# A fixed, searched order for the first two groups of an attention + MLP kernel, and the unread products at its end left out

## The chip, the cores and the metric

One core of a Trainium2 chip. The metric is the device time of the kernel in microseconds, the median of several runs. Five engines take part: TensorE (PE in the profile; its weight loads are PEld), VectorE (DVE), ScalarE (ACT), GpSimd (POOL) and SyncE (SP), which here issues almost every DMA. Each engine works through its own instructions in the order in which the program lists them; semaphores make one wait for another.

## The reference

Block-wise linear attention over q, k, v of shape (4, 8, 768, 64), all float32, with a decay per head, and then a two-layer MLP with leaky ReLU; the weights arrive as float64.

```
intra = einsum('bhic,bhjc->bhij', qb, kb) * Dmask          # scores, masked by lam**(i-j)
intra = einsum('bhij,bhjd->bhid', intra, vb)
inter = einsum('bhid,bhde->bhie', qb * lam_pow, kv_state)  # from the running state
kv_state = lam_block * kv_state + einsum('bhsd,bhse->bhde', kb_dec, vb)
...
x = attn_out.transpose(0, 2, 1, 3).reshape(3072, 512)
h = x @ w_in            # 512 -> 2048
g = maximum(0.01*h, h)
out = g @ w_out         # 2048 -> 512
```

## The kernel before, in words

The 3072 tokens are cut into 24 chunks of 128 (six per batch), and four chunks make a group of 512 tokens, so there are six groups. The 2048 hidden columns are cut into eight pairs p of 256.

Every float32 product of the MLP is made from three products of rounded parts: each operand is split into a high part h, a low part l and a mixed part m, and TensorE multiplies h by h, l by l and m by m. `up(g, p)` (L628 to L664) multiplies group g by weight pair p: two half blocks of 128 columns, three passes (h, l, m) of four 512-wide matmuls each, all on L640. Between l and m ScalarE scales the accumulator (L658), after m it applies the leaky ReLU into a buffer `gs` (L661), and a DMA stores `gs` to the DRAM array `g` (L664). The second half of the kernel, `down` (L700), reads these back and makes the output; nothing of it is touched by the change.

For chunk c the attention part is: load k, q, v (L338, L388); transpose k and q on TensorE (L403; four transposes each, here called Tk and Tq) and copy them out on ScalarE (L414, L415); scores (`go`) and state products (`kv`) on TensorE (L313); mask them (`sc`, L452) and update the running state (`st`) on VectorE (L457, L459) with POOL scaling between (L462); POOL or VectorE scales k (L419) and q (`qsT`, L423); outputs (`own`, then `inter` in two parts with a small probe read of `po` between, L491) on TensorE; and the split into xh (ScalarE, L507), xl and xm (VectorE, L508, L510). From chunk 10 on, q and k are not transposed on TensorE but loaded in 32 small strided pieces per run of chunks (`load_subs`, L374) and turned on VectorE.

A weight pair p arrives as two halves of float64 (L566, 512 KB each). ScalarE reads each half three times (L578, L580, L582), VectorE shifts and adds (L584, L585) to make float32, and `parts` makes wh (ScalarE L591 or VectorE L593), wl (VectorE L596) and wm (VectorE L602).

The order of all this is not written out by hand. The class `Plan` (L37 to L159) collects operations with an engine (or several to choose from), an estimated length, what they read and write as string keys, and a rank. `emit` then simulates the engines: again and again it takes the operation that can start first, ties broken by rank. An operation is known by its number in the order in which it was added. `seq` (L738 on) sets the ranks. At the start, where TensorE would sit idle by the plan's estimate, `busy` issues dummy transposes of 128x128 (L266) into the bank b10, until that bank is first used by a product. Before everything it issues eleven of them.

The steps that matter around the change, with their numbers: 71 to 73 load k3, q3, v3; 94 and 100 the two halves of the weights of p=1, 165 and 171 of p=0, 203 and 209 of p=2, 323 and 329 of p=4; 95 to 97 ScalarE's three reads of 94; 168 its third read of 165; 106, 177, 215, 335 make wh of p = 1, 0, 2, 4; 80 and 81 are kv and go of chunk 3, 87, 88, 90 its outputs, 91 its xh; 113 and 122 the transposes of q4 and q5; 154 the first pass of `up(0, 1)`; 243 the store of `up(0, 0)`; 266 the load of k8.

After the last operation the kernel issues 32 more matmuls that nobody reads: 24 in strips of the array (`strips`, L802) and eight small ones (L809).

Of the kernel before, what the change touches and what calls it, by code (L numbers as in the profile page):

```python
# [34 lines left out]


class Plan:  # L37

# [6 lines left out]
    def __init__(self):  # L45
        self.ops, self.last, self.rank = [], {}, 0.0
        self.chain, self.chains = None, {}
        self.warm, self.slack, self.more = 0.0, 0.0, {}
        self.first = {"PE": 0.0, "ACT": 0.0, "DVE": 3.4, "POOL": 0.0, "DMA": 0.2}
        self.cold, self.idle, self.spare = 6.0, None, None  # L50

    def begin(self, name):
# [30 lines left out]
    def emit(self):  # L83
        n = len(self.ops)
        follows, heads = {}, {}
        for c in self.chains.values():
# [26 lines left out]
        done = []  # L113
        while len(done) < n:
            best = None
            for e in free:
                for i in able[e]:
                    if e == "PE" and (i != locked[0] if locked else i in follows):
                        continue
                    t = max(free[e], since(i, e))  # L120
                    if (best is None or (t, self.ops[i][3]) < best[:2]) and good(i, e, t):
                        best = (t, self.ops[i][3], i, e)
            t, _, i, e = best
            ways, fn = self.ops[i][:2]
            if i in heads:
                locked = list(heads[i])
            elif locked and i == locked[0]:
                locked.pop(0)
            for x in ways:
# [8 lines left out]
            for u in users[i]:  # L138
                ends[u].append((free[e] + self.more.get(i, 0.0), e))
                left[u] -= 1  # L140
                if not left[u]:
                    for x in self.ops[u][0]:
                        able[x].add(u)
        self.timeline = sorted(done)

# [3 lines left out]
        for t, _, i, e in self.timeline:  # L149
            ways, fn, deps = self.ops[i][:3]  # L150
            t = max([soon[e]] + [over[d][0] + (0.0 if over[d][1] == e != "DMA" else self.SOON[over[d][1]]) for d in deps])
            if e == "PE":
                if self.spare in self.ops[i][4]:
# [9 lines left out]
def kernel(  # L163
# [32 lines left out]
    GOFIRST = 3  # L196
    SUBL, FIRST = 0.75, -8.0

    DV = 10
# [22 lines left out]

    W = [[sb([P, 4 * 2 * P], f"w{x}{p}", F32R) for x in "hlm"] for p in range(NP)]
    X = [[sb([P, KO, T], f"x{x}{i}", F32R) for x in "hlm"] for i in range(2)]
# [22 lines left out]
    kqv = [[x[:, i * H * D:(i + 1) * H * D].rearrange("p (h d) -> p h d", h=H) for i in range(2)] for x in kqv_f]  # L247
    kTs, qTs, qsTs = ([part(HP * C).rearrange("p (y t) -> p y t", y=HP) for _ in range(2)] for _ in range(3))
    sc = part(2 * HP * C2).rearrange("p (x y t) -> p x y t", x=2, y=HP)
    state = [part(HP * D).rearrange("p (y d) -> p y d", y=HP) for _ in range(4)]  # L250
# [75 lines left out]
    def of(c):  # L326
        return c // NCB, c % NCB, c % 2

# [98 lines left out]
    def scores(c):  # L427
# [17 lines left out]
        if c < GOFIRST:  # L445
            add("PE", 0.47, go, [f"kT{i}", f"qT{i}"], ["psc"])
        add("PE", 0.47, kv, [f"k{i}", f"v{i}"], ["psc"])
        if c >= GOFIRST:
            add("PE", 0.47, go, [f"kT{i}", f"qT{i}"], ["psc"])

        def uses():
            add("DVE", 0.69, lambda: nc.vector.tensor_tensor(sc, psc[:, :, lower, :], decay, op=ALU.mult), ["psc", "fk"], ["sc"])  # L452
            for t in range(n_pu):
                j = 2 * c + t
                new = state[j % 4]
                if n == 0 and t == 0:
                    add("DVE", 0.42, lambda new=new: nc.vector.tensor_copy(new, pu[0]), ["psc"], [f"st{j % 4}"])  # L457
                else:
                    add("DVE", 0.42, lambda new=new, t=t: nc.vector.tensor_tensor(new, new, pu[t], op=ALU.add),  # L459
                        ["psc"], [f"st{j % 4}"])  # L460
# [126 lines left out]
    def parts(p, src, keys):  # L587
        wh, wl, wm = W[p]
        def head(e):
            if e == "ACT":  # L590
                nc.scalar.activation(out=wh, in_=src, func=AF.Copy, bias=0.0, scale=NEAR / S)  # L591
            else:
                nc.vector.tensor_scalar(wh, src, NEAR / S, None, op0=ALU.mult)  # L593

        add(("ACT", "DVE"), (1.05, 0.7), head, keys, [f"wh{p}"])
        add("DVE", 1.25, lambda: nc.vector.scalar_tensor_tensor(wl, wh.bitcast(F32), -S, src, op0=ALU.mult, op1=ALU.add),  # L596
            keys + [f"wh{p}"], [f"wl{p}"])
        difference(p)

    def difference(p):  # L600
        wh, wl, wm = W[p]
        add("DVE", 1.25, lambda: nc.vector.scalar_tensor_tensor(wm, wl.bitcast(F32), 1.0, wh.bitcast(F32), op0=ALU.mult, op1=ALU.subtract),  # L602
            [f"wh{p}", f"wl{p}"], [f"wm{p}"])

    def w_in(p):
        for h in range(2):
            to_float32("wi", p, h, w32[:, h, :], f"w32{h}")
        parts(p, w32f, ["w320", "w321"])

# [153 lines left out]
    for n, x in enumerate(seq):  # L763
# [15 lines left out]
        elif x[0] == "wp":  # L779
            if not freed:  # L780
                add("DVE", 0.0, lambda: None, [], ATT + [f"gr{j}" for j in range(NR)])
                add("ACT", 0.0, lambda: None, [], [f"raw{j}" for j in range(NRAW)] + ["t0", "t1"])
# [5 lines left out]
        else:  # L788
            down(*x[1:])
    plan.emit()  # L790


    a, b = ring[0][0], W[0][0]
    spare = acc[0] + acc[1]

    def strips(n, times):

        k = P // n
        for _ in range(times):
            for i in range(n):  # L800
                r = slice(i * k, (i + 1) * k)
                nc.tensor.matmul(spare[i], lhsT=a[r, 0:P], rhs=b[r, 0:T], start=True, stop=True, skip_group_check=True)  # L802

    strips(2, 6)
    strips(4, 3)
    f = graw[0]
    for _ in range(4):
        for i in range(2):
            nc.tensor.matmul(spare[2][HALF[i], 0:C2], lhsT=f[:, 0:C2], rhs=f[:, 0:C2], start=True, stop=True, skip_group_check=True)  # L809

# [29 lines left out]
```

## Time and profile before

| what | value |
|---|---|
| median of 3 runs | 611.09 us (611.05 to 611.78) |
| profiled execution: span from first to last instruction | 610.3 us; its own time is not listed apart |
| TensorE busy | 601.9 us, 99% of the span |
| VectorE, ScalarE, POOL busy | 313.2, 269.9, 86.6 us |
| mean granted clock of TensorE | 0.997 |
| first product of `up` (L640) | 30.41 us after the start |
| dummy transposes (L266) | 30 |
| last product of `down` (L700) | issued by 606.3 us |
| DMA moved | 105.18 MB, 172 GB/s mean |

The profile names an instruction by engine, line and the tiles it writes and reads (`b<-xh,wh`). Busy time says where an engine had work; a wait says what ended an idle stretch; the chain of waits follows the last instruction back through what released each step. Rows by window give the busy microseconds of each engine in a stretch, the granted clock of TensorE (1.00 is full) and the share of the DMA engines in use.

### The profile page before, as it was taken

To read this page: it belongs to the slowest core of one execution; us is meant where nothing else is said; L and a number is where in the kernel's file an instruction comes from. 1 tells how busy PE (TensorE), PEld (TensorE's weight loads), DVE (VectorE), ACT (ScalarE), POOL (GpSimd) and SP (SyncE) were. 2 spreads that over 40 slices of the span, in tenths; PEclk is the share of its full clock that TensorE was granted. 3 is DMA by queue.
4 is the path that set the end of the run, shared out by engine and by line. 5 is a ranking of instruction groups with operands and counts; after the bars stand their busy time and mean duration, and the time that the engine had idled before them with its cause. 6 is when DMAs were issued, how large, how long until landed. Compare 5 with 4: busy or idle time off the path is not lost.

```text
span 610.3 us, 13012 instructions
## 1 busy us (share of the span) xinstructions
PE 601.9 (99%) x5426; PEld 497.6 (82%) x5426; DVE 313.2 (51%) x418; ACT 269.9 (44%) x430; POOL 86.6 (14%) x90
## 2 busy tenths in 40 slices
PE   7799999999999999999999999999999999999999
PEld 5688888888888878888788888888888888888887
DVE  5899764334243426326366755545454544636531
ACT  4678974444455646555577522222222313214111
POOL 2564412114133004104000000000000000000000
PEclk9899999999999999999999999999999999999999
DMA  9999775666889878886686843524333343333201
GB/s 201 236 261 263 215 204 126 175 154 176 192 212 245 212 222 219 212 242 212 233 302 219 278 155 103 173 69 139 137 104 134 111 136 111 132 104 126 82 1 69
DMA packets 147754, 105.18 MB, mean 172 GB/s; under 512 B 123632, under 2 KB 124400, under 8 KB 147696
## 3 DMA queue, kind: packets, MB, share of 16 engines
q1 hardware_dynamic: 147552, 104.36, 58.8%
q8 instruction: 42, 0.69, 0.5%
q14 instruction: 16, 0.13, 0.1%
q10 hardware_dynamic: 144, 0.00, 0.0%
HBM read 68.69 MB, written 35.65 MB: 171 GB/s over the span
## 4 chain that ended last, share of the span: by engine, by line
PE 95%; DMA 2%; ACT 1%; DVE 1%; issue 0%; SPq 0%; ACTq 0%
PE b L640 42%; PE b L700 18%; PE po L700 11%; PE psc L700 11%; PE po L313 4%; PE psc L313 4%; PE pt L700 4%; DMA g<-gs 1%; DMA att<-in_v_dram 1%; PE pt L403 1%; DMA att<-in_q_dram 1%; PE po L403 0%; PE psc L802 0%; ACT att L415 0%; PE b L266 0%
## 5 line engine op out<-in xcount | busy, mean ns | idle before, releaser
L682 ACT ACTIVATE xh<-att 128x1024 fp32r<-128x1024 f32 x48 | 50.8, 1060 | 149.1 <-PE b L700 133.6
L683 DVE SCALAR_TENSOR_TENSOR xl<-att,xh 128x1024 fp32r<-128x1024 f32 x48 | 58.7, 1223 | 97.5 <-ACT xh L682 97.5
L640 PE MATMUL b<-xm,wm 128*128 128x512 f32 (+2 forms) x392 | 104.5, 392 | 0.7 <-ACT b L658 0.7
L640 PE MATMUL b<-xh,wh 128*128 128x512 f32 (+2 forms) x392 | 103.2, 386 | 0.8 <-ACT xh L507 0.8
L640 PE MATMUL b<-xl,wl 128*128 128x512 f32 (+2 forms) x392 | 103.4, 387 | 0.0
L640 PEld LDWEIGHTS b<-xh,wh 128*128 128x128 f32 x392 | 72.9, 188 | 16.0 <-ACT xh L507 0.9
L640 PEld LDWEIGHTS b<-xl,wl 128*128 128x128 f32 x392 | 72.7, 188 | 15.1 <-DVE wl L596 0.3
L640 PEld LDWEIGHTS b<-xm,wm 128*128 128x128 f32 x392 | 71.4, 188 | 16.0 <-ACT b L658 1.1
L658 ACT ACTIVATE b<-b 128x512 f32<-128x512 f32 (+2 forms) x97 | 56.1, 580 | 60.6 <-PE b L640 60.5
L661 ACT ACTIVATE gs<-b 128x512 f32<-128x512 f32 (+2 forms) x97 | 57.0, 592 | 44.2 <-PE b L640 38.3
L700 PE MATMUL b<-wh,xh 128*128 128x512 f32 x192 | 74.7, 389 | 0.0
L700 PE MATMUL b<-wl,xl 128*128 128x512 f32 x192 | 74.7, 389 | 0.0
L685 DVE SCALAR_TENSOR_TENSOR xm<-xl,xh 128x1024 fp32r<-128x1024 f32 x48 | 58.7, 1225 | 4.7
L462 POOL TENSOR_TENSOR att<-att 128x256 f32<-128x256 f32 x40 | 34.4, 861 | 58.7 <-DVE att L459 58.7
L700 PEld LDWEIGHTS b<-wh,xh 128*128 128x128 f32 x192 | 36.1, 188 | 7.5
L700 PEld LDWEIGHTS b<-wl,xl 128*128 128x128 f32 x192 | 36.0, 188 | 7.5
L423 POOL TENSOR_TENSOR att<-att 128x512 f32<-128x512 f32 (+1 forms) x20 | 25.3, 1265 | 95.6 <-PE po L313 34.7
L452 DVE TENSOR_TENSOR att<-psc,att 128x512 f32<-128x512 f32 x24 | 16.5, 689 | 43.1 <-PE psc L313 43.1
L584 DVE TENSOR_SCALAR w<-w 128x512 int32<-128x512 int32 x32 | 19.6, 612 | 36.0 <-ACT w L578 35.9
L700 PE MATMUL psc<-wh,xh 128*128 128x512 f32 x96 | 37.3, 389 | 0.0
L700 PE MATMUL psc<-wl,xl 128*128 128x512 f32 x96 | 37.3, 389 | 0.0
L700 PE MATMUL psc<-wm,xm 128*128 128x512 f32 x96 | 37.3, 389 | 0.0
(79 smaller groups left out, 810.4 us busy)
## 6 DMA issues: line engine op xcount, KB each, us to landing
att<-g SPq DMA_DIRECT2D x48, 512.0 KB, 3.3
g<-gs SPq DMA_DIRECT2D x47, 512.0 KB, 4.0
raw<-in_moe_w_in_dram SPq DMA_DIRECT2D x16, 512.0 KB, 5.5
raw<-in_moe_w_out_dram SPq DMA_DIRECT2D x16, 512.0 KB, 4.8
att<-in_k_dram SPq DMA_DIRECT2D x48, 128.0 KB, 4.3
att<-in_v_dram SPq DMA_DIRECT2D x24, 256.0 KB, 4.5
out_dram<-gs SPq DMA_DIRECT2D x23, 256.0 KB, 2.1
wo<-w SPq DMA_DIRECT2D x8, 512.0 KB, 5.9
```

Source lines behind the costliest of these rows:

```text
L313: nc.tensor.matmul(dst[HALF[cols]], lhsT=lhsT[HALF[rows]], rhs=rhs[HALF[rows]], start=start, stop=True, skip_group_check=True)
L423: add(eng, us, lambda: e.tensor_tensor(o, x, _bc(pow_q, 2, 2)[:, :, m, :], op=ALU.mult), ["fq", dep], [f"qsT{i}"])
L452: add("DVE", 0.69, lambda: nc.vector.tensor_tensor(sc, psc[:, :, lower, :], decay, op=ALU.mult), ["psc", "fk"], ["sc"])
L462: add("POOL", 0.7, lambda new=new, j=j: nc.gpsimd.tensor_tensor(state[(j + 1) % 4], new, _bc(lam_c, 2, D), op=ALU.mult), [f"st{j % 4}", "f ...
L584: add("DVE", 0.42, lambda: nc.vector.tensor_scalar(d, d, 3, None, op0=ALU.logical_shift_left), [], [key])
L640: nc.tensor.matmul(dst, lhsT=w[z][:, kk * 2 * P + f * P:kk * 2 * P + (f + 1) * P], rhs=x[z][:, kk, toks], start=start and kk == 0, stop=kk ...
L658: add("ACT", ns, lambda b=b: nc.scalar.activation(out=b, in_=b, func=AF.Copy, bias=0.0, scale=S + 1.0), [], [kb], rank=-1.5)
L661: add("ACT", ns, lambda b=b, r=r: nc.scalar.activation(out=r, in_=b, func=AF.Prelu, bias=0.0, scale=1.0 / WS, alpha=0.01), [kb], [f"gs{jg} ...
L682: add("ACT", 1.05, lambda: nc.scalar.activation(out=h, in_=graw[j], func=AF.Copy, bias=0.0, scale=NEAR), reads, wr("h"))
L683: add("DVE", 1.25, lambda: nc.vector.scalar_tensor_tensor(l, graw[j], 1.0, h.bitcast(F32), op0=ALU.mult, op1=ALU.subtract), reads + [f"rh{ ...
L685: add("DVE", 1.25, lambda: nc.vector.scalar_tensor_tensor(m, l.bitcast(F32), -S, h.bitcast(F32), op0=ALU.mult, op1=ALU.add), [f"rh{j}", f" ...
L700: nc.tensor.matmul(acc[tb][z // 2][:, cols], lhsT=ring[j][z][:, f * T + tb * P:f * T + (tb + 1) * P], rhs=W[pp][z][:, f * d_model:(f + 1) ...
```

## The change

The 707 operations numbered 0 to 706 are no longer ordered by the plan. They are all operations that were added up to the last `up` of group 1: attention of chunks 0 to 11 and the products of chunk 12's round that belong to it, all eight weight pairs of w_in, all sixteen `up` of groups 0 and 1, and the loads for the turned chunks up to 15. A list, `ORDER`, gives their order; a suffix a, v or p picks ScalarE, VectorE or POOL where there is a choice, and `fN` puts N dummy transposes ahead of the next TensorE operation. `emit` first places the listed operations as they stand and then goes on by its old rule; the automatic dummies are off. What the list does to each engine's own order can be read off the numbers: on SP's queue q1 goes ahead of k1, 94 directly behind k1, v3 (73) directly behind k3, k8 (266) ahead of 323 and 329, 243 behind them. On TensorE go of chunk 3 goes ahead of kv, Tq of chunks 4 and 5 behind the outputs of chunk 3, and the chunks' rounds from 8 on stand at other places among the products. ScalarE reads 94 twice before the copy of chunk 1's k; 106, 177 and 215 are on ScalarE, 335 is on VectorE. Sixteen dummies are listed, where the plan had put in nineteen.

The key `psc` is split into `psS` (scores) and `psK` (state products), so the plan no longer orders these two against each other; `factors_q` reads the key it depended on. `OWN`, which would give some chunks buffers inside the weight tiles, is empty. The 32 unread matmuls at the end are gone.

```diff
+ORDER = """
+2 3 4 0 26 f3 5 25 9v f2 6 1 94 8 7 10 f5 11 12 28 14 48 13 15 29 95 32v 49 96 18 33 27 19 30 16 20a 31 100 17
+f1 21 50 22 34 23 51 72 36 52 53 55 24 54 97 f2 35 41 37 71 56 42 38 101 57 98 43a 102 73 44 39 104 45 58 40 59
+103 46 99 165 105 110 64 106a 60 75 171 61 65 77 74 109 66v 107 67 76 78 79 111 68 81 62 69 63 80 167 82 203 83
+f2 87 47 84 88 70 89a 166 f1 90 113 91 115 92 154 172 93 159 173 169 168 108 155 174 209 160 175 118 156 176
...
+"""
...
         for c in self.chains.values():
+            if first.intersection(c):
+                continue
...
+        for i, e in self.listed:
+            e = e or next(iter(self.ops[i][0]))
+            assert i in able[e]
+            put(i, e, max(free[e], since(i, e)))
+        while len(done) < n:
...
-                if self.idle is not None and t > soon[e] + 0.4:
+                if i in self.fill:
+                    self.idle(self.fill[i])
+                elif not self.listed and self.idle is not None and t > soon[e] + 0.4:
                     self.idle(int((t - soon[e] - 0.2) / 0.22))
...
-    add("DVE", 1.25, factors_q, [], ["fq"])
+    add("DVE", 1.25, factors_q, ["fk"], ["fq"])
...
-            add("PE", 0.47, go, [f"kT{i}", f"qT{i}"], ["psc"])
-        add("PE", 0.47, kv, [f"k{i}", f"v{i}"], ["psc"])
+            add("PE", 0.47, go, [f"kT{i}", f"qT{i}"], ["psS"])
+        add("PE", 0.47, kv, [f"k{i}", f"v{i}"], ["psK"])
...
+    for x in ORDER.split():
+        if x[0] == "f":
+            fill = int(x[1:])
+            continue
+        i = int(x.rstrip("avp"))
+        plan.listed.append((i, {"a": "ACT", "v": "DVE", "p": "POOL"}.get(x[-1])))
...
-    strips(2, 6)
-    strips(4, 3)
-    f = graw[0]
-    for _ in range(4):
-        for i in range(2):
-            nc.tensor.matmul(spare[2][HALF[i], 0:C2], lhsT=f[:, 0:C2], rhs=f[:, 0:C2], start=True, stop=True, skip_group_check=True)
```

More of the change, by code (lines that the diff above doesn't have):

```diff
@@ L37 @@
+694 664 698 671 702 661 682 699 703 672 704 676 700 695 679 705 683 660 662 666 674 706 657 652 678 656 681 677
+655
+"""
 class Plan:
@@ L50, in __init__ @@
         self.cold, self.idle, self.spare = 6.0, None, None
+        self.listed, self.fill = [], {}
     def begin(self, name):
@@ L85, in emit @@
         follows, heads = {}, {}
+        first = {i for i, _ in self.listed}
         for c in self.chains.values():
+            if first.intersection(c):
+                continue
             m = [i for i in c if "PE" in self.ops[i][0]]
@@ L113, in emit, with put @@
         done = []
[L114 to L123, printed above, removed]
+        def put(i, e, t):
             ways, fn = self.ops[i][:2]
[L125 to L128, printed above, removed]
             for x in ways:
@@ L197 @@
     SUBL, FIRST = 0.75, -8.0
+    OWN = {}
     DV = 10
@@ L326, in of @@
     def of(c):
-        return c // NCB, c % NCB, c % 2
+        return c // NCB, c % NCB, c % 2 if c not in OWN else 2 + list(OWN).index(c)
     pu = [psc[:, t, upper, :] for t in range(2)]
@@ L607, in w_in @@
             to_float32("wi", p, h, w32[:, h, :], f"w32{h}")
+        if p in OWN.values():
+            i = 2 + list(OWN.values()).index(p)
+            add("DVE", 0.0, lambda: W[p].__setitem__(slice(3), weights(p)), [],
+                [f"{x}{i}" for x in ("k", "q", "v", "kT", "qT", "qsT")] + [f"w{x}{p}" for x in "hlm"])
         parts(p, w32f, ["w320", "w321"])
@@ L780 @@
             if not freed:
-                add("DVE", 0.0, lambda: None, [], ATT + [f"gr{j}" for j in range(NR)])
+                add("DVE", 0.0, lambda: None, [], ATT + ["psS", "psK", "psc"] + [f"gr{j}" for j in range(NR)])
                 add("ACT", 0.0, lambda: None, [], [f"raw{j}" for j in range(NRAW)] + ["t0", "t1"])
```

76 lines of the change are left out of this document (56 added, 20 removed).

## The prediction

> **What bounds the kernel now.** I read the page first: the span, TensorE's busy time, the forty slices.
>
> ```profile
> span 610.3 us, 13012 instructions
> ...
> PE 601.9 (99%) x5426; PEld 497.6 (82%) x5426; DVE 313.2 (51%) x418; ACT 269.9 (44%) x430; POOL 86.6 (14%) x90
> ...
> PE   7799999999999999999999999999999999999999
> ```
>
> TensorE has work 99% of the span; only the first two slices (15.3 us each) show less. From the first real product on, nothing can be won but by fewer products or by filling holes. So I asked the waits: which holes are there, and how long?
>
> ```profile
> PE psc L313 <- DMA att<-in_v_dram: 1.8, 1, 1.8
> PE psc L313 <- DVE att L459: 1.6, 2, 1.1
> ...
> PE b L640 <- ACT xh L507: 0.8, 1, 0.8
> PE b L640 <- ACT b L658: 0.7, 1, 0.7
> ...
> PE po L313 <- ACT att L491: 0.3, 1, 0.3
> ```
>
> All but the last two (at 223.9 and 299 us) end before 30.41 us, where the first product of `up` starts. The other holes before that were filled with dummy transposes (L266). The chain of waits up to there, in order of time (start, length), says what holds that first product back:
>
> ```profile
> 19.07 5.23 DMA att<-in_v_dram
> 24.30 0.14 issue
> 24.43 1.57 PE psc L313 x64
> 26.00 1.26 PE b L266 x5
> 27.26 1.39 PE po L313 x48
> ...
> 29.86 0.51 ACT xh L507
> 30.36 0.04 issue
> 30.41 2.12 PE b L640 x8
> ```
>
> The load of v for chunk 3 (v3), issued at 19.07, lands at 24.30; its scores, five dummies, its outputs and xh follow. The same stretch by windows (PE, PEld, DVE, ACT, POOL busy; then granted clock, DMA share):
>
> ```profile
> 11.30:14.70 3.40, 2.32 (x78) 1.90 (x73) 2.91 (x5) 2.91 (x6) 0.62 (x1) 1.00 0.97 195
> ...
> 21.60:25.00 3.40, 1.61 (x57) 1.33 (x61) 2.31 (x4) 2.20 (x3) 3.40 (x4) 1.00 1.03 279
> 25.00:28.40 3.40, 3.40 (x91) 2.95 (x84) 2.35 (x4) 1.41 (x2) 1.02 (x2) 0.50 0.80 177
> ```
>
> ```profile
> 40.00:50.00 10.00, 10.00 (x150) 8.20 (x150) 9.76 (x13) 8.74 (x17) 3.97 (x3) 1.00 0.83 214
> 50.00:60.00 10.00, 10.00 (x171) 8.56 (x170) 9.53 (x14) 8.34 (x17) 5.58 (x4) 1.00 0.99 284
> ```
>
> Two readings. The clock is halved once, from 25.0 to 28.4, right after the emptiest stretch. And behind 30 us, where TensorE is full, VectorE is nearly so too: an earlier start of the products soon asks more of it. Last, the end:
>
> ```profile
> 606.29 2.02 PE psc L802 x14
> ...
> 608.76 0.62 PE po L809 x16
> ```
>
> **The change, part by part.** The sum is made against the profiled execution: its span of 610.3 stands 0.8 under the median of 611.09, and I take that 0.8 as unchanged.
>
> *No unused products.* L802 and L809 issue 32 matmuls whose results nobody reads; they run from 606.3 to 609.4. The last output store is issued at 607.25 and such half stores take 1.7 us to land (DMA issues from 600 us on), so 609.0. What is late next is that landing: the end moves by 0.4, not by 3.1. **-0.4** (bounds 0 and -0.5).
>
> *Loads.* Up to k3 the same transfers go first in both orders, and DMA is saturated (shares of 0.91 to 1.0 before 30 us), so k3 still lands at 20.0, where its transpose waited for it. Then v3 is next instead of q4 and v3: one load of 256 KB is about 1.2 us of the queue (210 GB/s), so v3 lands between 21.2 and 22.4 instead of 24.30. In exchange the first weight half goes ahead of v1: it lands 1.2 earlier (11.4 for 12.65), v1 at 14.8 for 10.4.
>
> *Chunk 1 gets later.* ScalarE's list has two conversions of that weight half (starts 0.58 and 0.65 apart) ahead of chunk 1's k copy (0.59), the probe of `po` (0.16) and the q copy: q is copied at 13.9, not 11.7. Its scores start at 13.96 (12.88 before); k2 and q2 transposes and two dummies (0.44 each) go ahead of kv1: 15.8 (13.37 before).
>
> *Chunk 2 catches up.* st2 (0.41), qsT2 (0.69), a shift (0.42) and st3 (0.41) on VectorE put kv2 at 18.3 (18.02 before); sc2 and xl1 (0.69 each, starts 0.60 apart) put own2 at 20.25 (20.39 before). The lateness ran into waits that were there anyway.
>
> *Chunk 3 gains.* VectorE then does the two low-word additions (0.68 each), st0 and the probe; ScalarE builds wh of p=1 (1.06) to 22.5 and copies q3 and k3 (0.59 each) to 23.5. go3, now ahead of kv3, starts at 23.5 (24.92 before, behind v3). VectorE reaches sc3 behind wl (1.65 beside POOL), qsT3, st1 and xl2, to 26.35; own3 starts at 26.4 (27.19), the last inter3 at 27.6 (29.16), xh3 runs 28.1 to 28.7 behind one conversion (0.68) in ScalarE's list. First product at **28.75 instead of 30.41: -1.66**.
>
> *What moved behind it.* The transposes of q5 (0.44) ran in a hole before and now run among the products: **+0.44**. The other transposes of chunks 4 and 5 keep their side of it. Sixteen dummies instead of nineteen: they fill holes in both, nothing.
>
> *30 to 60 us.* wh of p=0 and p=2 go from VectorE to ScalarE (mean 0.94 each on VectorE, 1.06 on ScalarE); wh of p=4 and p=7 come back later. Before, wl2 was ready 0.05 us ahead of its product (47.75 and 47.80), so 1.2 us earlier products need VectorE 1.2 us earlier there; the two heads give it 1.9. ScalarE, at 8.7 of 10, has 1.3 in that window. So the gain is kept: 0. If that cover is gone, every us of lateness is a us of TensorE. Two queues have new waits. SP stands at the second weight half of p=2 until ScalarE has read p=0's first half for the third time, about 31.0; k5, q5, k6 and v5 behind it then land from 35.6 to 39.2, and k5, the first one wanted, is wanted at 38.6. POOL scales k3 behind st1 and is done at 23.5; kv3 wants it at 25.2.
>
> *The split of the key psc, the key fk for factors_q, and OWN (empty)* alter which orders the plan admits, no instruction: 0.
>
> *Behind the list.* Group 2 is planned from where the list ends, with its chunk 15 loads already issued. The two later holes (0.7 at 223.9, 0.3 at 299 us) may go or be joined by others: I take 0, bounds -1.0 and +1.0.
>
> Sum: -1.66 + 0.44 - 0.4 = -1.6; 611.1 - 1.6 = **609.5**. The start alone has bounds of -3 (go3 right behind k3: 20.0 plus transposes 0.66, copy 0.59, scores 0.70, mask 0.69, outputs 0.93, probe 0.16, the rest 0.46, xh 0.60 is 24.8, of which half is likely lost in VectorE's queue) and +1 (chunk 1's lateness of 2.4 less the 1.4 that waits absorb).
>
> **The rivals.** *Half clock more often (610.5).* After the change TensorE sits idle from 11 to 13.4 us while ScalarE waits for the weight half: I count 1.5 us of work from 11.3 to 14.7, less than the 1.61 that preceded the half clock before. If an empty stretch of 3.4 us halves the next, 14.7 to 18.2 runs at half clock, and perhaps 25.0 to 28.4 as now. Price: kv with go took 1.57 there and 1.16 elsewhere, own with inter 1.46 and 0.93; about 0.5 a stretch, two stretches 1.0. Against it: the idle share that decides is not shown, and 2.32 of 3.40 did not do it. [...]
>
> *VectorE is the bound behind 30 us (610.6).* Products start earlier and then wait for wl and wm; only the end's 0.4 and a little stay. For it: 9.76 and 9.53 of 10 busy. Against: the two heads moved away, and PE needs nothing that is listed late.
>
> *Slower (612.7): the weights of p=4 stand behind a load that waits for TensorE.* Before, SP issued its two halves at 47.17 and 49.16, ahead of k8. The list puts k8 first, and k8 needs kv6 done (53.06; 51.5 with the gain): the halves issue at 52.5 and 53.0. At 5.5 us to landing (DMA issues of the page) they are there at 58.0 and 58.5; five conversions and additions among other work bring wh4 at 65.2 and wl4 near 66.7. The products want them at 66 and 66.9 (67.85 and 72.46 before, but the list pulls wl4 forward). No slack is left, so it decides from the landing on: each us later is a us lost, and beyond 2.8 us the change is slower than before by over 0.2%. Weight halves queued behind others took 7 us then; 10 would be needed.
>
> *Better (608.4):* the later holes go as well (-1.0).
>
> **How the numbers follow.** Likeliest, 0.48: 609.5, its own range 608.7 to 610.3 (0.4 either way for the pitches, 0.4 for wl2), a tenth of the whole lying above 609.87. Half clock 0.11, VectorE 0.10, slower 0.20, better 0.11. A measurement of this kernel (611.05 to 611.78) tells about 0.2%, 1.2 us, from no change: faster is 0.38 + 0.11 and a part of the two rivals around 610.5, 0.04, together 0.53; slower 0.20 and 0.02 for holes behind the list; the rest, 0.25, is the same. The range leaves out under a tenth at each end: 607.4 (start at its bound of -3, end -0.4, a third of the later holes) to 613.0 (the slow case and 0.3).
>
> **What would show it.** Right: the first product at 28.3 to 29.3, v3 no longer named by a wait of TensorE, the span ending with the store's landing 2.7 us after the last L700. Wrong: an own half clock in 14.7 to 18.2; L640 waiting for wl, wm or wh between 30 and 75 us, above all p=4; new waits of TensorE for gs or sc between 75 and 230 us, which a fixed order of 167 transfers on one queue could make and the plan's own order did not.

## The result and the profile after

The changed kernel takes 618.61 us (median; 617.33 to 619.80) against 611.07 (610.82 to 611.78) for the kernel before: a ratio of 1.0123, 95% interval 1.010 to 1.0146. It is slower by 7.5 us (1.2%); the prediction said 609.5, in a range up to 613.0.

The page of the changed kernel, span, busy time and slices:

```profile
span 617.9 us, 12896 instructions
...
PE 604.1 (98%) x5383; PEld 499.3 (81%) x5383; DVE 304.3 (49%) x419; ACT 267.5 (43%) x430; POOL 78.5 (13%) x89
...
PE   7899999999999999999999999999999999999997
...
PEclk9799999999999999999999999999999999999999
```

TensorE is busy for 2.2 us longer with 43 instructions less, and it is idle for longer too. (Line numbers: L313 before is L366 now, L403 is L456, L640 is L698, L661 is L719, L452 is L505, L459 is L512, L491 is L544.) The waits of TensorE, first from 11 to 34 us, then from 34 to 152 us, then from 152 us on (total, times, longest):

```profile
PE po L366 <- ACT att L544: 1.8, 1, 1.8
PE po L366 <- DVE xl L561: 1.4, 1, 1.4
PE psc L366 <- issue: 1.1, 2, 0.7
...
PE psc L366 <- DVE att L512: 1.1, 3, 0.4
PE psc L366 <- issue: 1.0, 1, 1.0
...
PE b L698 <- ACT gs L719: 0.8, 1, 0.8
```

v3 is no longer named, as predicted, but other waits took its place. Before, there was no wait at all between 30.4 and 223.9 us; now there are four, all in the attention rounds (`psc`). "issue" means that the view names nothing that ended the stop. The chain of waits for chunks 2 and 3:

```profile
19.42 0.68 PE psc L366 x29
20.10 0.43 issue
20.52 0.34 PE psc L366 x3
...
20.89 0.04 DVE att L505
...
22.23 0.69 PE po L366 x32
...
27.31 0.66 issue
27.97 1.17 PE psc L366 x32
29.14 0.02 issue
29.16 0.70 DVE att L505
...
33.53 2.55 PE b L698 x11
```

kv2 runs at 19.42, stops inside for 0.43, and only after its end does the mask sc2 (L505) start; own2 follows at 22.23. kv3 starts at 27.97, sc3 again only after it. The first product stands at 33.2 us, 2.8 later than before.

The "issue" of 0.66 us ahead of kv3 is a wait all the same, for VectorE's state add (L512):

```profile
27.45 0.42 DVE L512 TENSOR_TENSOR att<-att,psc 128x256 f32<-128x256 f32 x1 [1.05 <-PE psc L366]
...
27.97 1.13 PE L366 MATMUL psc<-att 64*64 64x64 f32 x32 [0.66 <-issue]
```

and TensorE's queue at a semaphore ahead of it (length in ns, start in us):

```profile
L366 PEldq EVENT_SEMAPHORE  x1: 1447/1447/1447, 26.5 to 26.5; - x1
```

This is the second state add of chunk 2, operation 62. The list has it behind go3 and ahead of kv3 (`81 62 69 63 80`). It reads the states' half of the tile `psc`, but it waited for the end of go3 (27.31), which writes the scores' half. TensorE's queue stood at a semaphore from 26.47 to 27.92, until the add was done (27.87), and kv3 followed. In the kernel before, this add comes ahead of both kv3 and go3.

The same stretch of the start by windows (PE, PEld, DVE, ACT, POOL busy; granted clock, DMA share):

```profile
12.88:16.30 3.42, 3.38 (x49) 3.26 (x50) 1.89 (x3) 1.66 (x3) 0.63 (x1) 0.50 1.07 293
...
40.00:50.00 10.00, 10.00 (x192) 8.46 (x184) 8.14 (x12) 9.20 (x17) 7.06 (x6) 1.00 0.92 228
```

The stretch from 12.88 to 16.30 is at half clock (granted 0.50), and so are 23.1 to 33.4 (0.50): four stretches of 3.41 us where the kernel before had one. From 40 to 50 us VectorE is less busy than before (8.14 of 10 against 9.76): it is not the bound.

To see where the loss arises I compared the two traces at points where TensorE has done the same set of operations. After minus before: +3.2 us at 45 us, +3.35 at 62, +3.8 at 72, +4.4 at 114, +5.2 at 126, +5.8 at 135, +7.6 at 155, +8.0 at the last `up` product, and +7.6 at the end of the span. So two stretches lose: the start (3.2) and the attention rounds from 62 to 152 us (4.4). In the second, the time from `own` of a chunk to the next product, and the order inside, was:

```
chunk   before: own inter kv go inter    after
5       2.02                             2.12  own inter go inter kv
6       2.17                             2.62  own inter kv inter go
8       2.02                             2.07  own go inter kv inter
9       2.03                             2.63  own inter kv inter go
10      2.02                             2.62  own go inter kv inter
11      2.03                             3.31  own inter go inter kv
4, 7    2.02                             2.02  own inter kv go inter (as before)
```

Only rounds in a new inner order got longer. The timeline of the round of chunk 6 (start, length, idle time before and what ended it):

```profile
64.33 0.45 PE L366 MATMUL po<-att 64*64 64x64 f32 x8
64.67 0.42 DVE L512 TENSOR_TENSOR att<-att,psc 128x256 f32<-128x256 f32 x1 [2.83 <-PE psc L366]
65.15 0.69 PE L366 MATMUL psc<-att 64*64 64x64 f32 x32 [0.37 <-DVE att L512]
```

go7 writes the scores' half of the tile `psc`; it waits 0.37 us until VectorE has read the states' half (the state add, L512).

### The profile page after: what moved, and what is told of

It reads as the page before. It is cut to its first block, busy times and chain, and to the rows that moved or that the text cites. A ratio compares the mean times of both kernels' runs of the same rounds, so it can differ in the third digit from the quotient of the medians.

```text
span 617.9 us, 12896 instructions
## 1 busy us (share of the span) xinstructions
PE 604.1 (98%) x5383; PEld 499.3 (81%) x5383; DVE 304.3 (49%) x419; ACT 267.5 (43%) x430; POOL 78.5 (13%) x89
## 4 chain that ended last, share of the span: by engine, by line
PE 95%; ACT 1%; issue 1%; DMA 1%; SPq 1%; DVE 1%; DVEq 0%; ACTq 0%
PE b L698 43%; PE b L758 18%; PE po L758 11%; PE psc L758 11%; PE po L366 4%; PE psc L366 4%; PE pt L758 4%; DMA raw<-in_moe_w_in_dram 1%; PE pt L456 1%; SPq L391 1%; PE po L456 0%; PE b L456 0%; DVE att L512 0%; ACT low L633 0%; ACT gs L719 0%
## 5 line engine op out<-in xcount | busy, mean ns | idle before, releaser
L698 PE MATMUL b<-xh,wh 128*128 128x512 f32 (+2 forms) x392 | 104.0, 390 | 0.9 <-ACT gs L719 0.8
L698 PE MATMUL b<-xm,wm 128*128 128x512 f32 (+2 forms) x392 | 103.6, 393 | 0.0
L698 PE MATMUL b<-xl,wl 128*128 128x512 f32 (+2 forms) x392 | 102.6, 388 | 0.0
L698 PEld LDWEIGHTS b<-xh,wh 128*128 128x128 f32 x392 | 72.0, 188 | 17.1 <-ACT gs L719 2.5
L698 PEld LDWEIGHTS b<-xl,wl 128*128 128x128 f32 x392 | 72.7, 188 | 16.1 <-issue 1.3
L698 PEld LDWEIGHTS b<-xm,wm 128*128 128x128 f32 x392 | 71.1, 188 | 16.0 <-ACT b L716 1.7
L716 ACT ACTIVATE b<-b 128x512 f32<-128x512 f32 (+1 forms) x97 | 55.9, 582 | 59.6 <-PE b L698 59.5
L719 ACT ACTIVATE gs<-b 128x512 f32<-128x512 f32 (+2 forms) x97 | 56.9, 592 | 48.6 <-PE b L698 41.8
L512 DVE TENSOR_TENSOR att<-att,psc 128x256 f32<-128x256 f32 x40 | 16.6, 414 | 64.5 <-PE psc L366 63.4
L515 POOL TENSOR_TENSOR att<-att 128x256 f32<-128x256 f32 x40 | 27.6, 690 | 107.8 <-DVE att L512 69.2
L366 PE MATMUL po<-att 64*64 64x64 f32 x1472 | 35.6, 229 | 3.7 <-ACT att L544 2.1
L366 PEld LDWEIGHTS po<-att 64*64 64x64 f32 x1472 | 29.0, 140 | 12.1 <-issue 6.6
```

The lines of the kernel that those rows point to most:

```text
L366: nc.tensor.matmul(dst[HALF[cols]], lhsT=lhsT[HALF[rows]], rhs=rhs[HALF[rows]], start=start, stop=True, skip_group_check=True)
L698: nc.tensor.matmul(dst, lhsT=w[z][:, kk * 2 * P + f * P:kk * 2 * P + (f + 1) * P], rhs=x[z][:, kk, toks], start=start and kk == 0, stop=kk ...
L716: add("ACT", ns, lambda b=b: nc.scalar.activation(out=b, in_=b, func=AF.Copy, bias=0.0, scale=S + 1.0), [], [kb], rank=-1.5)
L719: add("ACT", ns, lambda b=b, r=r: nc.scalar.activation(out=r, in_=b, func=AF.Prelu, bias=0.0, scale=1.0 / WS, alpha=0.01), [kb], [f"gs{jg} ...
```

## The experiments

All ratios below are to the kernel before, with 95% intervals. "Row" counts TensorE's matmuls and weight loads from the start of the trace.

### e1: the list with the kernel before's own order

```
 ORDER = """
-2 3 4 0 26 f3 5 25 9v f2 6 1 94 8 7 10 f5 11 12 28 ...
+2 3 4 0 25 26 1 5 27 7 9v 6 94 8 10 f3 11 49 f3 12 28 ...
```

> The changed kernel with the 707 listed operations put in the order that the kernel before had for them (its fills of idle time too); the split key, the absent unused products and the list itself stay. Theory A (the loss is in the order of the listed operations): TensorE goes as before to the end of the second group, about 150 us, and the run takes 610 to 611.5 us. Rival B (the loss comes from what follows a list: operations outside the 707 are pushed behind it, the plan then continues from another state): 614 us or more, and the difference from the kernel before opens only behind the last listed operation.

Measured: 614.13 us, 1.0054 (1.0034 to 1.0074). Rival B's mechanism is what happens, and 2.8 us is its price: at 62 us TensorE stands where it stands in e5 below (+0.1), and still does at 160 us; then the difference opens: +1.7 at 171 us, +2.2 at 249, +3.3 at the last `up`, with the first new wait behind the list. TensorE's waits from 152 us on:

```profile
PE b L698 <- ACT gs L719: 1.1, 2, 0.8
PE b L698 <- ACT b L716: 0.7, 1, 0.7
PE b L698 <- ACT xh L560: 0.3, 1, 0.3
PE po L366 <- ACT att L544: 0.3, 1, 0.3
```

A list that ends after two groups changes what the plan makes of the rest, even where the list holds the plan's own order.

### e2 and e3: half of the list each

```
e2:  before's order up to operation 162 (the last pass of up(0, 1)), then the new order
e3:  the new order up to operation 162, then before's order
```

> The listed operations up to the first completed block of up products in the kernel before's order, the rest in the new order. In the two traces the start accounts for +3.3 us (read at 45 to 63 us) and the stretch from 63 to 152 us for +4.3. Theory A (two separate losses): 618.6 - 3.3 = 615.3 us, range 614.3 to 616.3. Rival (the middle's loss hangs on a start that is late): 612 us or less.

> The other half of e2: the new order up to the same block, then the kernel before's order. Theory A (separate losses): 618.6 - 4.3 = 614.3 us, range 613.3 to 615.3. Rival (the middle's loss is made by the new order's start, through what that leaves for VectorE): 617 us or more.

Measured: e2 615.35 us, 1.0064 (1.0049 to 1.0079), as theory A has it. e3 622.49 us, 1.0184 (1.0169 to 1.0199): 8 us above what the separate losses give. The rival's "617 us or more" holds, but VectorE is only half of what the waits name. e3's waits of TensorE from 34 to 60 us:

```profile
PE pt L456 <- DMA att<-in_q_dram: 2.1, 2, 1.9
PE b L698 <- DVE wl L650: 1.8, 1, 1.8
```

The new start issues q5's load at 35.9 us instead of 22.3, and the old continuation wants it earlier. Against e5 below, e3 is 3.4 us late at its first product, 8.5 at 49 us, still 8.4 at 160 and 12.2 at the last `up`. So the old rounds lose nothing in themselves; the loss is made where the old order meets the new start (5 us), and behind the list (3.8, as in e1, whose list ends in the same order). The new middle runs behind the old start (e2) at about the cost that the comparison above gave.

### e4: the rounds put back

```
-188 189 187          go6 inter5 kv6
+187 188 189          kv6 go6 inter5
...
-273 275 274          kv7 inter6 go7
+273 274 275          kv7 go7 inter6
```

and the like for the rounds of chunks 8, 9, 10 and 11; the other engines' orders are untouched.

> The changed kernel with one edit in TensorE's order: in the rounds of chunks 5, 6, 8, 9, 10 and 11 the state products and the scores of the next chunk follow each other again, as own, inter, kv, go, inter; all other engines' orders are the same. Theory A (the tile of scores and states is one thing for the waits: what writes one half waits for the reader of the other half, so that a round in the new order takes 2.07 to 3.31 us where the old one takes 2.02): the rounds go back to 2.02 to 2.05 us each, the sum of their excess of 3.1 us goes, and the run takes 615.5 us, range 614.7 to 616.3. Rival B (those rounds were late because VectorE was; the same wait comes back in front of or behind the round): 617.5 to 619 us, as the changed kernel.

Measured: 617.51 us, 1.0102 (1.0087 to 1.0117). The mechanism is as theory A says; the time is in rival B's range, and the runs (617.04 to 618.49) overlap those of the changed kernel. The three waits for L512 are gone, and over the rounds of chunks 5 to 10 TensorE gains 1.7 us on the changed kernel (1.35 ahead at 32 us, 3.04 ahead at 126). The 1.35 are no work of the edit: the start is the same, but the profiled run of e4 has one stretch at half clock in it, that of the changed kernel four. The timeline of the round of chunk 6 in e4:

```profile
63.39 0.34 PE L366 MATMUL po<-att 64*64 64x64 f32 x4
63.65 1.19 PE L698 MATMUL b<-xm,wm 128*128 128x512 f32 x4
63.69 0.42 DVE L512 TENSOR_TENSOR att<-att,psc 128x256 f32<-128x256 f32 x1 [3.52 <-PE psc L366]
```

VectorE reads while products run, and nobody waits. In the round of chunk 11 the repair only moved kv12 ahead of its data; the round takes 3.78 us, with the one wait of TensorE from 60 to 152 us:

```profile
PE psc L366 <- DMA att<-in_v_dram: 1.5, 1, 1.5
```

### e5: the kernel before without the unused products

```
-    strips(2, 6)
-    strips(4, 3)
-    f = graw[0]
-    for _ in range(4):
...
```

> The kernel before without the unused products behind the plan, and nothing else; every engine's order is that of the kernel before. The same program also comes out when all 1,948 operations are listed in the kernel before's order, so that beside e1 it prices what the plan makes behind a list that ends after two groups. Theory A: TensorE's last used product ends as before, the end comes 0.4 us earlier, 610.6 to 611.0 us; e1 (614.13) lost its 2.8 us over the kernel before behind its list. Rival B: 613 us or more, the list and the products' absence cost in themselves.

Measured: 611.14 us, 0.9996 (0.9984 to 1.0008). Rival B is out; the 0.4 us of theory A are less than the interval, so the times can't tell them from nothing. Two things come with it. Its profile has no half clock before the last 3 us, and its first product stands at **28.6 us**, in the order in which the profile before showed 30.4. And e1 lost 3.0 us against it, all behind the list.

### e6: more unused transposes in the start

```
-f1 21 ... 64
+f13 21 ... f8 64
```

> The changed kernel with 12 more unused transposes ahead of the second half of inter0 and 8 ahead of own2, where TensorE stands 1.8 and 1.4 us; all else as it is. Theory A (the half clock comes of TensorE's idle time at 11 to 23 us): no stretch at half clock in any run, granted clock 0.999 to 1.000; with 0.8 us for each of the one to four stretches that the changed kernel's runs hold, 616.0 to 616.9 us, and runs that agree within 0.7. Rival B (the stretches come whatever TensorE does there): clock 0.988 to 0.997 and 617.3 to 619.8 us. Apart from that: the stop without a wait inside kv2 stands at row 698 of TensorE's matmuls and loads (698 too in e3 and e4, whose row count ahead is the same). If it is tied to the place in the program, as code that is fetched late would be, it moves to 24 rows earlier work, which is the first half of kv2 or its start; if it is tied to kv2's operands it stays at kv2's last rows.

Measured: 617.39 us, 1.0098 (1.0083 to 1.0113). No half clock in the profiled run, one stretch in one of the others: theory A on the clock, and still only 1.2 us below the changed kernel. That is above theory A's range. What took the rest is in its waits from 17 to 24 us and from 270 to 285 us:

```profile
PE psc L366 <- issue: 1.5, 1, 1.5
...
PE b L698 <- issue: 1.0, 1, 1.0
```

The stop in kv2 is at row 698 again, with 24 rows more ahead of it; it is 1.5 us long now and stands in kv2's middle. It goes with the row, not with kv2's last rows. In each case it ends about 1.5 us after a 16 KB packet on the DMA queue that the page calls "instruction". Stops of this kind in several kernels:

```
kernel   row                   at                 goes on at   packet ended   later by
after     698 = 2*256 + 186    end of kv2           20.52        19.05         1.47
e4        698                  end of kv2           20.84        19.35         1.49
e6        698                  middle of kv2        21.46        20.09         1.38
e11       698                  first row of kv2     21.76        20.27         1.49
e9        955 = 3*256 + 187    go3                  24.31        22.67         1.64
e11      1970 = 7*256 + 178    in a round           57.83        56.43         1.40
after    4005 = 15*256 + 165   end of kv12         139.28       137.80         1.48
e6       7320 = 28*256 + 152   a product           279.83       278.24         1.59
e10      8086 = 31*256 + 150   end of a round      302.65       301.25         1.40
e11      8086                  end of a round      303.26       301.88         1.38
```

The wait ahead of kv3 shown above is not of this kind: it is at row 912, and the last such packet had ended 3.7 us earlier. The rows of the table lie at steps of 256 with a slow drift, and the queue shows the same step: the page counts 42 of these packets for the 10,766 matmuls and weight loads of the changed kernel, one for 256 of them, and in the kernel before each packet from 356 us on begins 256 rows after the one ahead of it. Most of them go by without a stop: the changed kernel's trace has the two of the table for its 42 packets. A stop was 0.3 to 1.7 us long, mostly where TensorE ran through short matmuls. That TensorE stood until the packet's content was there is my reading of rows and packets; no view names what ended a stop. e6 shows that the stop stays at the row and does not go with the operation.

### e7: the masks ahead of the state products

```
+    plan.ops[58][2].add(59)     # kv2 depends on sc2
+    plan.ops[80][2].add(82)     # kv3 depends on sc3
```

> The changed kernel with the mask of the scores of chunks 2 and 3 (sc2, sc3) recorded ahead of the state products kv2 and kv3, by one dependence each; the order of every engine is the same, only what waits for what differs. Theory A (the two halves of the tile of scores and states are one thing for the waits, so that sc2 waits for kv2 which it does not read): sc2 starts at go2's end (18.6 to 19.0 us) instead of 20.9 to 21.2, sc3 at go3's end (26.2) instead of 29.1, kv2 now waits for sc2's read (to about 19.9), own2 begins by 21.3 instead of 22.2 to 22.5, own3 0.5 to 0.9 us sooner after kv3, and the first up product comes 1.0 to 2.0 us sooner: 615.5 to 616.8 us. Rival B (VectorE is late for another reason): sc2 at 20.9 or later still, time as the changed kernel's, 617.3 to 619.8.

Measured: 616.88 us, 1.0092 (1.0077 to 1.0107), just above theory A's range, and its runs (616.55 to 618.06) overlap those of the changed kernel; the mechanism is A's, as the trace shows. sc2 and its neighbours, in the changed kernel first:

```profile
20.89 0.69 DVE L505 TENSOR_TENSOR att<-psc,att 128x512 f32<-128x512 f32 x1 [1.20 <-PE psc L366]
21.50 0.68 DVE L561 TENSOR_TENSOR xl<-po,xh 128x512 fp32r<-128x512 f32 x1
...
22.23 0.34 PE L366 MATMUL po<-att 64*64 64x64 f32 x8 [1.38 <-DVE xl L561]
```

and in e7:

```profile
19.54 0.69 DVE L505 TENSOR_TENSOR att<-psc,att 128x512 f32<-128x512 f32 x1
20.14 0.68 DVE L561 TENSOR_TENSOR xl<-po,xh 128x512 fp32r<-128x512 f32 x1
20.33 0.69 PE L366 MATMUL psc<-att 64*64 64x64 f32 x32 [1.32 <-POOL att L515]
...
20.88 0.52 PE L366 MATMUL po<-att 64*64 64x64 f32 x20
```

With the recorded order of sc2 and kv2 exchanged and every engine's order the same, sc2 starts 1.35 us sooner and without a wait for TensorE (1.20 us in the changed kernel); own2 comes at 20.88. So sc2 had waited for kv2, whose result it does not read. Whether it is the shared tile that makes the dependence is not tested: two separate tiles for scores and states were not tried.

### e8, e10, e11: the repairs together, and with the idle time filled

```
e8:   e7's two dependences, e4's rounds for chunks 5 to 10, and
 VectorE
-59 46 99 105 60 66 107 79 62 69 82
+59 60 46 99 105 66 79 82 62 69 107
 POOL
-40 61 78
+40 78 61
e10:  e8 and   +f5 57   +f5 58   +f9 64   +f4 81   +f5 80
e11:  e10 and  f5 11 -> f10 11   f1 21 -> f11 21   f2 35 -> f5 35   f5 58 -> f6 58
```

> The changed kernel with three repairs of its list: the rounds of chunks 5, 6, 8, 9 and 10 as own, inter, kv, go, inter (chunk 11's round stays); sc2 and sc3 recorded ahead of kv2 and kv3; on VectorE the state add of chunk 2 straight behind sc2, and sc3 and the next state add ahead of xl2 and wl1; on POOL the scaling of k3 ahead of a state's decay. Theory A (the loss is the sum of what the runs named): to e7's 616.9 us the rounds give -1.7, and kv3 starts at 26.0 instead of 26.7, so that the first up product comes at 30.2 to 30.7 (31.1 in e7) for another -0.6: 614.6 us, range 613.8 to 615.4. [...] Rival B (each repair uncovers the next wait): 616.5 us or more.

> The kernel of e8 with 28 unused transposes in TensorE's idle places from 17 to 28 us (5 ahead of the second half of inter1, 5 ahead of kv2, 9 ahead of own2, 4 ahead of go3, 5 ahead of kv3); every other engine as in e8. e8's runs held 13.65 us at half clock from 20.8 us on, its first up product stood at 34.2 us, and its time was 618.5. Theory A (the half clock is what undid e8's repairs): no half clock before 40 us, first up product at 30.0 to 31.0 us, and 615.2 us, range 614.4 to 616.2; the stop without a wait stays at TensorE's row 698, now in the middle of kv2, 0.8 to 1.5 us long. Rival B (the repairs are undone by the next wait at any clock): first up product at 32 us or later and 617 us or more.

> The kernel of e10 with 19 more unused transposes ahead of kv2 (5 ahead of go0, 10 ahead of inter0's second half, 3 ahead of kv1, 1 ahead of kv2), all put where TensorE stands idle, so that its row 698 is the first of kv2 and not in kv2's middle. Theory A (the stop is code that has not arrived, tied to a place in the program): the stop coincides with the wait that stands ahead of kv2 anyway, no stop is left inside kv2, own2 comes 0.5 to 1.2 us sooner after kv2's first row, and the time is 0.4 to 1.0 us below e10's, as far as no other crossing of this kind is met. Rival B (the stop belongs to kv2's or own2's data): it is still inside kv2, and the time is e10's or above, since the added transposes can only delay.

Measured: e8 618.52 us, 1.0125 (1.0103 to 1.0148); e10 617.91, 1.0096 (1.0078 to 1.0113); e11 619.75, 1.0128 (1.011 to 1.0145). Three misses; rival B is right in e8 and e10. In e8 and e10, the window from 20.8 to 34.4 us:

```profile
20.80:34.40 13.60, 10.89 (x211) 8.52 (x208) 7.92 (x14) 4.63 (x8) 3.26 (x4) 0.50 0.65 173
```

```profile
20.80:34.40 13.60, 11.70 (x264) 9.14 (x265) 9.70 (x17) 6.75 (x13) 3.49 (x5) 1.00 0.66 178
```

All of it at half clock in e8, none of it in e10. But e10 has a stretch at half clock of its own, earlier, where e8 has none:

```profile
13.65:17.06 3.41, 3.41 (x58) 2.96 (x54) 1.89 (x3) 1.89 (x4) 1.53 (x1) 0.50 1.05 285
```

At the end of kv2 e8 is 1.15 us ahead of e10; at the first product (34.2 against 32.8) it is 1.5 behind. So e8's four stretches cost about 2.7 us, 0.7 each, as an estimate: e10's added transposes in that window are not taken out. The start of e4 against that of the changed kernel, the same order with one stretch instead of four, gives the same: 1.35 us earlier although its stop in kv2 is 0.7 longer, so 0.7 each. In the end e10 gains only 0.6, since other things happen on the way: kv12 waits 1.3 us for v12, and a stop of 0.8 without a wait stands at 302 us.

The clock does not explain why kv3, expected at 26.0 us in e8, comes at 29.25:

```profile
28.17 0.69 DVE L505 TENSOR_TENSOR att<-psc,att 128x512 f32<-128x512 f32 x1 [2.44 <-PE psc L366]
28.78 0.41 DVE L512 TENSOR_TENSOR att<-att,psc 128x256 f32<-128x256 f32 x1
...
29.25 1.03 PE L366 MATMUL psc<-att 64*64 64x64 f32 x28 [1.14 <-DVE att L512]
```

go3 ends at 28.10, sc3 (28.17) waits for it, the state add of chunk 2 stands behind sc3 on VectorE, and kv3 waits for the state add. e10 has the same chain at full clock, with kv3 at 28.78. The repair made it longer, since it put sc3 ahead of kv3. At row 698 e10 has no stop: it starts kv2 at 21.26, 1.6 us after the packet had ended. In e11 the stop at row 698 fell on kv2's first row, as theory A placed it, but it was longer than the wait that it was to hide in: of the 2.1 us, the wait for a semaphore was over at 20.18, and 1.6 came behind it (waits of TensorE, 17 to 24 us):

```profile
PE psc L366 <- issue: 2.1, 1, 2.1
```

The packet that ended ahead of it began at 19.0 us there instead of 18.3 in e10 and 18.1 in the changed kernel. What sets the moment at which a packet is sent I can't read from the traces; that stays open. Two more things made e11 the slowest of the three: its profiled run has one stretch at half clock behind kv2 (23.2 to 26.6 us), and the stop at row 8086 was 1.7 us long.

### e9: v3 ahead of q4, alone, in the kernel before's order

```
-110 73 ... 113 80 81        load q4, load v3 ... Tq4 kv3 go3
+73 110 ... 80 81 113        load v3, load q4 ... kv3 go3 Tq4
```

> The kernel before's order throughout, listed whole and without the unused products, with one exchange on two queues: v3's load ahead of q4's, and kv3 and go3 ahead of the transposes of q4. That is the one gain of the start that the prediction named, alone. In e5 TensorE waits 0.7 us for q4 and 0.8 us for v3 at 22.1 to 23.8 us. Theory A (that wait is on the path to the first product): v3 lands at 22.6 instead of 23.6, the first up product comes at 27.6 to 28.0 us instead of 28.6, and 610.2 to 610.6 us against e5's 611.1. Rival B (VectorE, which makes xl3, wl1 and wm1 for the next products, is late next and takes it back): the first product comes sooner, the second wait grows by as much, 610.9 to 611.4 us.

Measured: 611.55 us, 1.0005 (0.9996 to 1.0014): no gain, and the first product at 29.5 us, 0.9 later than in e5. v3 lands at 21.85 (23.61 in e5) and kv3 starts at 22.86 (23.75), so 0.9 is won there. It is lost at once: go3 stops at row 955 for 0.4 us without a wait, the transposes of q4 now come behind go3, and own3 starts at 25.82 (25.71 in e5). The rest is lost on ScalarE, which stands for the transposes of q4, in the unchanged order of its work:

```profile
25.38 0.59 ACT L468 COPY att<-pt 128x512 f32<-128x512 f32 x1 [2.57 <-PE pt L456]
```

Behind this copy come a wh and two conversions of weights, and only then, at 28.09 us (26.71 in e5), the probe of `po` for which the second half of inter3 waits. Neither theory foresaw a later first product. kv3's own wait has a new name, k3's scaling:

```profile
PE psc L366 <- POOL att L472: 0.7, 1, 0.7
```

### e12: e2 with the kernel before's order behind the list

```
 ORDER = """ ... (e2's 707 operations)
+ ... (the other 1,241 operations in the kernel before's order)
```

> The list of e2 (the kernel before's order to the first block of up products, then the new order), followed by all operations behind it in the kernel before's order; the plan chooses nothing. In every kernel whose plan continues behind the list (the changed one, e1 to e4, e6 to e8) TensorE waits 0.8 us for a gs copy at 335 to 344 us, and against e5 the difference grows by 0.9 to 1.3 us behind 150 us. Theory A (the prediction's step 'behind the list', taken as 0, is a cost of the plan continuing from another state): that wait is not there, TensorE's difference from e5 at 150 us (3.6 to 3.9) stays to the end of the up products, and the time is 614.0 to 614.6 us, e2's 615.35 less 0.9 to 1.3. Rival B (the later wait is a product of lateness itself, and the kernel before's order makes one too, as in its own profile at 223.9 us): 615.0 to 615.6 us.

Measured: 614.24 us, 1.0045 (1.0029 to 1.006): theory A. The difference from e5 is 3.9 us at 146 us and 3.9 at the last `up`; e2's grew to 4.8. One wait of TensorE is left from 152 us on:

```profile
PE po L366 <- ACT att L544: 0.3, 1, 0.3
```

## Why the prediction was wrong

**The base.** "0.8 under the median" was wrong. In every run of every kernel here the time is 1.73 to 1.86 us above its span. The profiled execution of the kernel before (span 610.3) was thus one of 612.1 us, 1.0 above the median, and its half clock at 25.0 to 28.4 us is not in every execution. Without it the same start has its first product at 28.6 (e5), 28.7 (e2) and 29.1 us (e1). Of the 1.8 us between the profiled execution and e5, 0.7 were there before the half clock: v3 landed at 24.30 us in the one and at 23.61 in the other, in the same order. The predicted 28.75 is, by e5, what the kernel before already did in most executions.

**The start: -1.66 predicted, +2.8 at the first product (+4.6 against e5), +3.2 by 45 us.** The loads were right: the weight half landed at 11.03 (11.4 predicted), v1 at 14.63 (14.8), v3 at 22.11 (21.2 to 22.4). So was chunk 1's beginning: go1 at 13.41 (13.96). The failed step is *Chunk 2 catches up*, and *Chunk 3 gains* with it: sc2 was taken to follow the scores. It follows kv2 (20.89 instead of about 19), behind a half clock, and behind a stop inside kv2 that no view of the kernel before had shown at such a length. In the kernel before sc2 waits for kv2 too (0.23 us, to 19.04), but two sets of transposes run meanwhile; the list puts own2 straight behind. kv3 then came at 27.97 (25.2) and own3 at 29.91 (26.4). The prediction counted go3 ahead of kv3 as a gain; with one tile it made the state add wait for go3 and kv3 for the state add, 0.66 us of TensorE here and 1.14 in e8. This is read from the traces; no run takes that order out alone. v3, on whose wait the gain was built, gives nothing in the old order either (e9). The half clock is a part only: without any, the changed start has its first product at 31.9 us (e6), 3.3 later than e5.

**The key split: "no instruction: 0".** This is the step that missed the rounds. It admits orders in which scores and state products of a chunk stand apart, while the tile stayed one. In the rounds of chunks 6, 9 and 10 the second writer waits for VectorE's read (0.34 to 0.38 us each); taking that order out gave 1.7 us over the rounds of chunks 5 to 10 (e4). With chunk 11's round (1.28 longer, of which 1.03 is the stop at row 4005) the six rounds account for 3.1 of the 4.4 us lost from 45 us to 152.

**The moved transposes: +0.44.** The reading is right: at the first product four transposes fewer are done than in e5 (36 and 40). No run prices them alone. From the first product to the point where 48 are done, e7 and e5 both take 12.2 to 12.3 us, and e5 waits 0.4 us in it, so about 0.4 more work is there, and the time is the same.

**30 to 60 us: 0.** Right: +3.2 at 45 us, +3.35 at 62. VectorE was not the bound, and the slower rival named the wrong mechanism: no product waited for the weights of p=4, though the change ended on that rival's side.

**Behind the list: 0, bounds -1.0 and +1.0.** Inside the bounds, by luck. Continuing from a list costs 1.1 us in e2 (e12 takes it back) and 3.0 in e1. In the changed kernel it shows as the 0.8 us wait at 342.1, and only because the kernel before's wait at 223.9 is gone is the net +0.4.

**The dummies: "nothing".** Their count also shifts which operation stands at a row where TensorE stops: row 698 is at kv2's end in the changed kernel, in its middle in e6 and its first in e11, and the stops there were 0.43, 1.5 and 1.6 us long.

**The half clock.** The rival named the stretch that came (14.7 to 18.2 predicted, 12.88 to 16.30 seen) and nearly its price (0.5; 0.7 by e8 and e10), but with a chance of 0.11, and as a gain lost. By the mean clocks it came one to four times a run: the changed kernel's runs with 0.988 and 0.992 took 619.8 us, those with 0.997 took 617.4. So it explains the 2.4 us between these runs and a part of the loss; those at 617.4, with about one stretch as the kernel before has at the same 0.997, are still 6.3 us above the kernel before. In the two traces the stretches of the start are 3.41 us long (25.0 to 28.4 before, 12.88 to 16.30 after) or three of that in a row (23.1 to 33.4), and the mean clocks of the changed kernel's four runs go from 0.988 to 0.997. What decides where a stretch falls no run shows.

**The end: -0.4.** Right. From the last used product to the end of the span: 4.0 us before, 3.6 after.

What stays open: the start's 3.2 us are not taken apart into sums. The halves (e2, e3, e12) place the loss, and e4 and e7 show two of its causes at work, but repairs in the list (e8, e10, e11) moved the loss to other waits and did not lower it. No version beat the kernel before; e5 and e9 equal it.

## What to carry to other kernels

Before a planner's resource is split, check that the waits the program really makes split with it: a key that is finer than the tile buys orders whose cost the plan cannot see. Subtract the span from the time in several runs before the sum is built on one profiled execution; here a clock stretch and a late load of that one execution were booked as the change's gain. And an order that came out of a search is good only with what stands around it: half of it, or the plan's own continuation behind it, cost up to 8 us more than the parts read alone.

## What the runs showed of the hardware that was not expected

- TensorE stopped without a semaphore to wait for: 0.3 to 1.7 us long, at rows that are multiples of 256 apart up to a slow drift, each stop ending 1.4 to 1.6 us after a 16 KB packet on the instruction queue. They hit mostly stretches of 64x64 matmuls (32 of them start within 0.47 us), now and then a product.
- Half clock: a start with 10.9 us of work in 13.6 ran at 0.50 throughout (e8), while one with 11.7 ran at 1.00 (e10); a stretch of 3.41 us cost about 0.7 us there, by an estimate.
- The time of a run stands 1.73 to 1.86 us above its span in every kernel here, with or without unused products at the end.
